# Query projection in halves of the array's rows, and sums in the output banks, in an attention kernel with two MLPs

## The chip, the cores and the metric

The kernel runs on one core of a Trainium2 chip. TensorE (PE) does the matmuls and writes to PSUM, which has eight banks of 512 float32 columns on 128 partitions; VectorE (DVE), ScalarE (ACT) and GpSimd (POOL) do the rest, and DMA queues, most of them issued by SyncE (SP), move data. Each engine works through its own list of instructions in order, and semaphores tell one of the others' progress. The metric is the device time of one execution in microseconds (us), lower is better.

## The reference

```python
def phi(x):                                   # q, k, v: (4, 8, 576, 64), w_phi: (64, 128)
    proj = np.einsum('bhsd,df->bhsf', x, w_phi)
    proj = proj - np.max(np.abs(proj), axis=-1, keepdims=True)
    return np.concatenate([np.exp(proj), np.exp(-proj)], axis=-1)
q_p, k_p = phi(q), phi(k)
kv = np.einsum('bhsf,bhsd->bhfd', k_p, v)
z = np.sum(k_p, axis=2)
num = np.einsum('bhsf,bhfd->bhsd', q_p, kv)
den = np.einsum('bhsf,bhf->bhs', q_p, z)[..., None] + 1e-06
attn_out = num / den                          # then (2304, 512): heads side by side
h = x @ w_in                                  # first MLP, 512 -> 2048 -> 512
x = np.maximum(0.01 * h, h) @ w_out
h = x @ w_in                                  # second MLP, with mish instead
x = (h * np.tanh(log1p(exp(h)))) @ w_out
```

The weights of the MLPs arrive as float64 and are turned into float32 on the chip, by integer operations on VectorE.

## The kernel before, in words

**Attention.** The 32 (batch, head) pairs are worked through two heads at a time, 16 units with index i. Of the 576 rows of a head 512 are the main part and 64 the left rest; the rests of several heads are put together. A head pair takes these steps, each with its own function: `transposes` brings queries and keys with the head dimension to the partitions (four 128x128 transposes each, even and odd rows on either half of the partitions; for an even i two more for the rests of two pairs); `split` makes of each a rounded high part (ScalarE, `hi`) and the remainder (VectorE, `lo`), so that `three` can multiply in three passes (lines 84 to 86). `q_proj` and `k_proj` project; the weight `wbd` has zeros on one half of its rows, so that a whole-array matmul picks the even or the odd rows. The queries come out with the features on the partitions: ScalarE copies them to `qd` (L403), GpSimd takes the maximum over the partitions (L408), `q_guard` subtracts it (L412). `k_guard` does it for the keys on VectorE (L365, L366). ScalarE makes the exponentials `kp`, `lp` (rests) and `qp`, each with either sign (L388). `kv` multiplies keys and values (L425, L428), with the column of ones that gives the sum; each matmul uses half of the array's columns, two are queued next to each other. `kv_copy` (L434) takes the sums out of the bank `kvp`. `nd` (L448, L453) makes numerators and denominators in the two banks `outs`; `normalise` (L461 to L464) divides on VectorE into `xn`, and `x_left` (L474) the left rows on ScalarE into `xleft`. `x_t` transposes `xn` into the bank `xt` (L482) and the left rows, by a matmul with two identities added, into a part of the next `kvp` (L484); ScalarE copies both to `X` (L485, L490).

**Order.** It is written out by hand: each engine works in the order in which the code issues. `attention(n)`, called turn n here, n = 0 to 16, works on five pairs at once: it normalises and transposes the outputs of pair x = n - 2, makes the outputs of o = n - 1, the exponentials and the sums of w = n, the projections of p = n + 1 and the input transposes of t = n + 2. In turn 15 the steps `moe(0)` and `moe(1)` of the first MLP are put in, in turn 16 and after it the third, and after that the MLPs run alone.

**PSUM.** Four banks are a ring, `bank("a")`, from which the projections and the input transposes take a bank in turn; `outs` has two banks, `kvp` one and `xt` one. For the MLPs the last four become the second ring.

**Conversion.** `Conv` turns one unit of weights (128x512) at a time. In turn n, `begin` clamps and shifts (L134, L136), `scale` multiplies on ScalarE (L150), `join` puts the bits together (L159, L162), and for the first ten units `split` in the next turn makes the two parts that stay in SBUF (L215, L216). Of the other 22 units of the first MLP five are converted in the turns and stored to HBM for later (`kept`, "store"), and fetched again in the first MLP block; the other 17 are converted there, by `step`, twice for each of the block's 14 items from item 2 on (L196, L198, L199, L205, L177, L215, L216).

**MLP.** For an item (128 hidden columns by 512 tokens) `emit_h` issues twelve matmuls, `leaky` makes the activation and its split (L663 to L670, `g`, `gh`, `gl`), and `emit_o`, two items later, twelve more.

Of the kernel before, what the change touches and what calls it, by code (L numbers as in the profile page):

```python
# [23 lines left out]
def attention_two_mlps_kernel(  # L24
# [12 lines left out]
    nc = tc.nc  # L37
# [18 lines left out]


    Q_COL = ((HM, 0, HM + P, P), (HM + LEFT, LEFT, HM + LEFT + P, LEFT + P))
# [160 lines left out]
    kept = rest[:17:4]  # L219
# [31 lines left out]
    with tc.manual_schedule():  # L251
# [3 lines left out]
        xleft = [ap.tile([P, 2, D], F32, name=f"xleft{i}", bufs=1) for i in range(2)]  # L255
        nc.vector.memset(xleft[0], 0.0)
# [8 lines left out]
        vleft = [ap.tile([P, 2, D + 1], F32, name=f"vleft{i}", bufs=1) for i in range(NV)]  # L265
        for i in range(NV):
            nc.vector.memset(vmain[i][:, :, :, D:D + 1], 1.0)
            nc.vector.memset(vleft[i], 0.0)
            for r in range(2):
                nc.vector.memset(vleft[i][r * LEFT:(r + 1) * LEFT, r, D:D + 1], 1.0)  # L270
        nc.vector.memset(xleft[1], 0.0)

        fold = ap.tile([P, LEFT], F32, name="fold", bufs=1)
        nc.vector.tensor_tensor(out=fold, in0=ident[:, 0:LEFT], in1=ident[:, LEFT:2 * LEFT], op=ALU.add)
# [3 lines left out]
        nc.vector.memset(outs[:, 0, 4 * (D + 1):5 * (D + 1)], 1.0)  # L278
# [30 lines left out]
        def values(i):  # L309
            b, p = divmod(i, NP)  # L310
            h0 = 2 * p
            vm = st[i]["vm"] = vmain[i % NV]
            for h in range(2):
                nc.sync.dma_start(out=vm[:, h, :, 0:D], in_=v[b, h0 + h, 0:MAIN, :].rearrange("(p t) d -> p t d", t=NM))
            vl = st[i]["vl"] = vleft[i % NV]
            for r in range(2):
                nc.sync.dma_start(out=vl[r * LEFT:(r + 1) * LEFT, r, 0:D], in_=v[b, h0 + r, MAIN:S, :])
# [5 lines left out]
        zeros = xleft[0].rearrange("p h d -> p (h d)")  # L323
# [6 lines left out]
        def transposes(i, *parts):  # L330

            s = st[i]
            l = lf[i // 2]
            for nm in parts or "qlk":
                if nm != "l":
                    t = bank("a")
                    for j in range(NM):  # L340
                        nc.tensor.transpose(
                            out=t[:, j * P:(j + 1) * P],
                            in_=s[nm + "n"].rearrange("p h t d -> p (h t d)")[:, j * P:(j + 1) * P], identity=ident)
                    n = HM if nm == "k" else HM + LEFT
                    hi, lo = (ap.tile([P, 2, n], F32R, tag=f"{nm}t{x}", name=f"{nm}t{x}", bufs=1) for x in "hl")
                    s[nm + "h"], s[nm + "l"] = (x.rearrange("p h n -> p (h n)") for x in (hi, lo))
                    split(hi[:, :, 0:HM], lo[:, :, 0:HM], t.rearrange("p (h n) -> p h n", h=2))
                elif i % 2 == 0:
                    t = bank("a")
# [5 lines left out]
                    split(l["h"], l["l"], t[:, 0:2 * P])  # L355

        def q_left(i):
            s, l = st[i], lf[i // 2]
            c = P + (i % 2) * LEFT
            for x in "hl":  # L360
                nc.vector.tensor_copy(out=s["q" + x][:, HM:HM + LEFT], in_=l[x][:, c:c + LEFT].bitcast(F32))
# [7 lines left out]
        def k_proj(i, c):  # L369
            s = st[i]  # L370
            if c == 0:
                s["kd"] = ap.tile([P, 2, NM, F], F32, tag="kd", name="kd")
            t = bank("a")
            for j in range(2):
                u = slice((2 * c + j) * P, (2 * c + j + 1) * P)
                three(t[:, j * 2 * F:(j + 1) * 2 * F], s["kh"][:, u], s["kl"][:, u], wbh, wbl)
            k_guard(t.rearrange("p (n f) -> p n f", f=F), NM, s["kd"][:, c])

        def k_proj_left(i):
            l = lf[i // 2]  # L380
            l["kd"] = ap.tile([P, 2, F], F32, tag="kdl", name="kdl", bufs=1)
            t = bank("a")
            three(t[:, 0:2 * F], l["h"][:, 0:P], l["l"][:, 0:P], wbh, wbl)
            k_guard(t[:, 0:2 * F].rearrange("p (n f) -> p n f", f=F), 2, l["kd"])
# [6 lines left out]
        def q_proj(i, c):  # L391
            s = st[i]
            h, o = divmod(c, 2)
# [3 lines left out]
            t = bank("a")  # L397
            n = HM + (h == o) * LEFT
            c0 = h * (HM + (1 - o) * LEFT)
            d0 = (1 - o) * (HM + h * LEFT)  # L400
            f = slice(o * F, (o + 1) * F)
            three(t[:, 0:n], wbh[:, f], wbl[:, f], s["qh"][:, c0:c0 + n], s["ql"][:, c0:c0 + n])
            nc.scalar.activation(out=s["qd"][:, h, d0:d0 + n], in_=t[:, 0:n], func=AF.Copy)  # L403
            half = s.setdefault("half", set())
            half.add(c)
            if {2 * h, 2 * h + 1} <= half:
                qd, qm = s["qd"][:, h, :], s["qm"][:, h, :]
                nc.gpsimd.partition_all_reduce(qm, qd, P, bass_isa.ReduceOp.absmax)  # L408
# [5 lines left out]
        def kv(i, a):  # L414

            s, l = st[i], lf[i // 2]
            if a == 0:
                s["kvp"] = pa.tile([P, 512], F32, tag="kvp", name="kvp")
            both = s["kvp"][:, 0:4 * (D + 1)].rearrange("p (h a n) -> p h a n", h=2, a=2)


            for h in range(2):
                for t in range(NM):
                    for r in HALVES:
                        nc.tensor.matmul(out=both[r, h, a, :], lhsT=s["kp"][a][:, h, t, r], rhs=s["vm"][:, h, t, :],  # L425
                                         start=(a == 0 and h == 0 and t == 0), stop=False, skip_group_check=True)
            for r in HALVES:
                nc.tensor.matmul(out=both[r, :, a, :], lhsT=l["lp"][a][:, i % 2, r], rhs=s["vl"],  # L428
                                 start=False, stop=(a == 1), skip_group_check=True)

        def kv_copy(i):
            s = st[i]
            s["kv"] = ap.tile([P, 4, D + 1], F32, tag="kv", name="kv", bufs=1)
            nc.scalar.activation(out=s["kv"], in_=s["kvp"][:, 0:4 * (D + 1)].rearrange("p (c n) -> p c n", n=D + 1), func=AF.Copy)  # L434

        def nd(i):

            s = st[i]
            N = D + 1
            t = s["nd"] = outs  # L440
            g = t[:, :, 0:4 * N].rearrange("p c (u h n) -> p c u h n", u=2, h=2)

            for u in range(NM):
                for h in range(2):
                    q0 = Q_COL[h][u]
# [5 lines left out]
            for a in range(2):  # L451
                for h, r in enumerate(HALVES):
                    nc.tensor.matmul(out=t[r, 1, 4 * N:5 * N], lhsT=s["qp"][a].rearrange("p h n -> p (h n)")[:, MAIN + r.start:MAIN + r.stop],  # L453
                                     rhs=s["kv"][:, 2 * h + a], start=(a == 0), stop=(a == 1))

        def normalise(i):
            s = st[i]
            N = D + 1
            t = s["nd"]
            den = s["den"] = ap.tile([P, 2, 5], F32, tag="den", name="den")  # L460
            nc.vector.tensor_scalar(out=den, in0=t[:, :, D:5 * N:N], scalar1=1e-6, scalar2=None, op0=ALU.add)  # L461
            nc.vector.reciprocal(out=den, in_=den)
            s["xn"] = ap.tile([P, NM, 2, D], F32, tag="xn", name="xn")
            nc.vector.tensor_tensor(  # L464
                out=s["xn"].rearrange("p (c u) h d -> p c (u h) d", c=2),
                in0=t[:, :, 0:4 * N].rearrange("p c (m n) -> p c m n", n=N)[:, :, :, 0:D],
                in1=den[:, :, 0:4].unsqueeze(3).to_broadcast([P, 2, 4, D]), op=ALU.mult)
            s["xl"] = xleft[i % 2]

        def x_left(i):  # L470

            s = st[i]
            for h, r in enumerate(HALVES):
                nc.scalar.activation(out=s["xl"][r, h], in_=s["nd"][r, 1, 4 * (D + 1):4 * (D + 1) + D], func=AF.Copy,  # L474
                                     scale=s["den"][r, 1, 4:5])

        def x_t(i):
            s = st[i]
            b, p = divmod(i, NP)
            t = pa.tile([P, 512], F32, tag="xt", name="xt")  # L480
            for j in range(NM):
                nc.tensor.transpose(out=t[:, j * P:(j + 1) * P], in_=s["xn"][:, j].rearrange("p h d -> p (h d)"), identity=ident)  # L482
            o = st[min(i + 1, PAIRS - 1)]["kvp"][:, MAIN - LEFT:MAIN]
            nc.tensor.matmul(out=o, lhsT=s["xl"].rearrange("p h d -> p (h d)"), rhs=fold, start=True, stop=True)  # L484
# [13 lines left out]
        def start():  # L498
# [6 lines left out]
            q_left(0)  # L505
            q_proj(0, 1)
            q_proj(0, 2)
            k_proj(0, 1)
            q_proj(0, 0)
            q_proj(0, 3)  # L510
# [8 lines left out]
        def attention(n):  # L519
# [23 lines left out]
            if w is not None:  # L543
                k_exp(w, 0)
# [24 lines left out]
            if p is None:  # L569
                normalise(o)  # L570
                x_left(o)
# [266 lines left out]
```

## Time and profile before

| | us |
|---|---|
| median of 3 runs | 969.28 (967.63 to 969.98) |
| the profiled execution | 967.76 |
| its span | 965.9 |
| TensorE busy | 950.6 (98%) |
| VectorE busy | 711.6 (74%) |
| ScalarE busy | 505.2 (52%) |
| GpSimd busy | 68.5 (7%) |

The span goes from the first to the last instruction that was profiled. Busy time is the union of an engine's instructions; matmuls overlap one another in the pipeline, so one lasts longer than the distance to the next, and it is the distances of starts that add up. Attention takes the first 182 us, the two MLPs the rest.

### The profile page before, as it was taken

The numbers are of one execution on the slowest core, as the hardware profiler recorded it, in microseconds if no ns is written. First come the engines' busy times: TensorE is split into PE (matmuls) and PEld (weight loads), VectorE is DVE, ScalarE is ACT, GpSimd is POOL, SyncE is SP. The second block draws the span as 40 slices with busy tenths as digits, with TensorE's granted clock in tenths as the row PEclk, the third lists the DMA queues.
The fourth block names the chain that finished last, engine by engine and source line by source line (L and its number), as shares of the span: only waits on it lengthen the run. The fifth ranks groups of instructions, "written<-read, shape, count | busy, mean of one in ns | idle before, by whom it ended". The sixth has DMA issues, their size and how long they took to land.

```text
span 965.9 us, 16740 instructions
## 1 busy us (share of the span) xinstructions
PE 950.6 (98%) x6704; PEld 813.9 (84%) x6704; DVE 711.6 (74%) x1271; ACT 505.2 (52%) x882; POOL 68.5 (7%) x36
## 2 busy tenths in 40 slices
PE   8999999999999999999999999999999999999998
PEld 7888999888888899888888888888888988888886
DVE  7999997599656575765344569778878689778875
ACT  6889998555433333432334456455445455445443
POOL 4433533000000000000000000000000000000000
PEclk9999999999999999999999999999999999999999
DMA  7444543255224444443012210001000100001001
GB/s 207 130 123 132 163 130 92 88 158 168 67 87 142 148 136 140 137 150 131 0 44 88 88 65 1 0 1 44 1 1 1 44 1 23 1 0 44 1 1 44
DMA packets 68206, 72.97 MB, mean 76 GB/s; under 512 B 27169, under 2 KB 52641, under 8 KB 68129
## 3 DMA queue, kind: packets, MB, share of 16 engines
q1 hardware_dynamic: 67392, 71.52, 23.8%
q8 instruction: 52, 0.85, 0.4%
q10 hardware_dynamic: 736, 0.39, 0.1%
q14 instruction: 26, 0.20, 0.1%
HBM read 57.48 MB, written 14.42 MB: 74 GB/s over the span
## 4 chain that ended last, share of the span: by engine, by line
PE 85%; DVE 9%; ACT 5%; POOL 1%; issue 1%; DMA 0%; POOLq 0%; ACTq 0%; DVEq 0%
PE a L84 14%; PE a L85 14%; PE a L86 14%; PE b L84 14%; PE b L86 14%; PE b L85 14%; DVE qd L412 1%; DVE mx L365 1%; ACT kp L388 1%; DVE kd L366 1%; DVE xn L464 1%; POOL qm L408 1%; ACT qp L388 1%; DVE wl L216 1%; PE outs L448 1%; PE kvp L425 1%
## 5 line engine op out<-in xcount | busy, mean ns | idle before, releaser
L84 PE MATMUL a<-wh,wh 128*128 128x512 f32 (+1 forms) x640 | 235.7, 368 | 0.0
L86 PE MATMUL a<-wh,wl 128*128 128x512 f32 (+1 forms) x640 | 235.4, 368 | 0.0
L85 PE MATMUL a<-wl,wh 128*128 128x512 f32 (+1 forms) x640 | 235.4, 368 | 0.0
L84 PEld LDWEIGHTS a<-wh,wh 128*128 128x128 f32 x640 | 120.6, 188 | 20.7 <-issue 0.3
L85 PEld LDWEIGHTS a<-wl,wh 128*128 128x128 f32 x640 | 120.7, 189 | 20.2
L86 PEld LDWEIGHTS a<-wh,wl 128*128 128x128 f32 x640 | 120.6, 188 | 20.0
L670 DVE TENSOR_TENSOR gl<-g,gh 128x512 fp32r<-128x512 f32 x72 | 49.9, 693 | 110.3 <-ACT gh L667 110.3
L84 PE MATMUL b<-gh,wh 128*128 128x512 f32 (+1 forms) x320 | 117.8, 368 | 0.8 <-ACT X L490 0.8
L85 PE MATMUL b<-gl,wh 128*128 128x512 f32 (+1 forms) x320 | 117.7, 368 | 0.0
L86 PE MATMUL b<-gh,wl 128*128 128x512 f32 (+1 forms) x320 | 117.7, 368 | 0.0
L84 PE MATMUL b<-wh,gh 128*128 128x512 f32 x288 | 112.2, 389 | 0.0
L85 PE MATMUL b<-wl,gh 128*128 128x512 f32 x288 | 112.2, 389 | 0.0
L86 PE MATMUL b<-wh,gl 128*128 128x512 f32 x288 | 112.1, 389 | 0.0
L667 ACT ACTIVATE gh<-g 128x512 fp32r<-128x512 f32 x72 | 45.5, 632 | 116.1 <-PE b L86 110.9
L692 ACT ACTIVATE gh<-u 128x512 fp32r<-128x512 f32 x72 | 45.5, 632 | 70.4 <-PE b L85 63.7
L666 DVE TENSOR_TENSOR g<-g,a 128x512 f32<-128x512 f32 x72 | 49.4, 687 | 42.8 <-ACT g L663 40.0
L408 POOL PARTITION_ALL_REDUCE qm<-qd x32 | 68.3, 2184 | 91.3 <-ACT qd L403 77.7
L719 ACT ACTIVATE r<-e,two 128x512 f32<-128x512 f32 x72 | 51.7, 718 | 36.3 <-DVE e L704 36.3
L84 PEld LDWEIGHTS b<-gh,wh 128*128 128x128 f32 x320 | 60.4, 189 | 10.9 <-ACT X L490 0.9
L86 PEld LDWEIGHTS b<-gh,wl 128*128 128x128 f32 x320 | 60.4, 189 | 10.0
L85 PEld LDWEIGHTS b<-gl,wh 128*128 128x128 f32 x320 | 60.3, 189 | 9.9
L688 ACT ACTIVATE e<-a 128x512 f32<-128x512 f32 x72 | 43.0, 597 | 47.9 <-PE a L86 26.6
(118 smaller groups left out, 1621.1 us busy)
## 6 DMA issues: line engine op xcount, KB each, us to landing
stage<-in_moe_w_in_dram SPq DMA_DIRECT2D x32, 512.0 KB, 3.8
stage<-in_moe_w_out_dram SPq DMA_DIRECT2D x32, 512.0 KB, 3.6
scr<-c SPq DMA_DIRECT2D x37, 256.0 KB, 2.0
wstage<-scr SPq DMA_DIRECT2D x32, 256.0 KB, 3.4
qn<-in_q_dram SPq DMA_DIRECT2D x16, 256.0 KB, 4.6
vmain<-in_v_dram SPq DMA_DIRECT2D x32, 128.0 KB, 3.5
kn<-in_k_dram SPq DMA_DIRECT2D x15, 256.0 KB, 4.3
out_dram<-X SPq DMA_DIRECT2D x15, 256.0 KB, 2.1
```

What stands on the lines that cost most here:

```text
L84: nc.tensor.matmul(out=o, lhsT=wh_, rhs=xh, start=start, stop=False)
L85: nc.tensor.matmul(out=o, lhsT=wh_, rhs=xl, start=False, stop=False)
L86: nc.tensor.matmul(out=o, lhsT=wl_, rhs=xh, start=False, stop=stop)
L216: return lambda: nc.vector.tensor_tensor(out=lo, in0=src, in1=hi.bitcast(F32), op=ALU.subtract)
L388: nc.scalar.activation(out=e, in_=src, func=AF.Exp, scale=float(sg))
L408: nc.gpsimd.partition_all_reduce(qm, qd, P, bass_isa.ReduceOp.absmax)
L666: nc.vector.tensor_tensor(out=g, in0=g, in1=h, op=ALU.max)
L667: nc.scalar.activation(out=hi, in_=g, func=AF.Copy)
L670: nc.vector.tensor_tensor(out=lo, in0=g, in1=hi.bitcast(F32), op=ALU.subtract)
L688: nc.scalar.activation(out=e0, in_=h0, func=AF.Exp)
L692: nc.scalar.activation(out=hi2, in_=u2, func=AF.Copy)
L719: nc.scalar.activation(out=r0, in_=e0, func=AF.Ln, bias=two)
```

## The change

- `q_proj` works on a whole head (both the even and the odd rows) in one call: six matmuls, of 64 rows of the array each, alternating between the upper half with one bank and the lower half with the other. One copy of 576 columns takes both out.
- A tile of two banks (`pair_of_banks`, one buffer) holds these projections, and also the transposes of queries and keys, which are split together, 1024 columns at once, into one tile `qk` for each part. In a turn three steps use it one after the other.
- `kv` writes its sums behind the outputs in the two `outs` banks instead of `kvp`, and the left rows' products use 64 rows by 64 columns of the array each, without zeros in `vleft`.
- `normalise` takes the left rows along (640 columns); `x_left` and its tiles are gone. `x_t` transposes the left rows by two matmuls of 64 rows by 64 columns into `outs`, and the rest into a bank of the ring; the bank `xt` is gone.
- In a turn the order is now first query head, `normalise`, keys, first exponential of the keys, second query head, left keys.
- Three units are stored for later instead of five; the two others are converted in the first MLP block.

```diff
@@ -54,8 +54,10 @@
-    Q_COL = ((HM, 0, HM + P, P), (HM + LEFT, LEFT, HM + LEFT + P, LEFT + P))
+    Q_COL = (0, HM + LEFT, P, HM + LEFT + P)
+    N = D + 1
+    KV0 = 5 * N
...
-    kept = rest[:17:4]
+    kept = rest[2:15:6]
...
+        def pair_of_banks():
+            return pa.tile([P, 2, 512], F32, tag="two", name="two").rearrange("p b n -> p (b n)")
+        qk = {x: ap.tile([P, 4, HM + LEFT], F32R, name=f"qk{x}", bufs=1) for x in "hl"}
...
+            both = None if parts else pair_of_banks()
             for nm in parts or "qlk":
+                g = "qk".find(nm)
                 if nm != "l":
-                    t = bank("a")
+                    t = bank("a") if parts else both[:, g * 2 * HM:(g + 1) * 2 * HM]
...
+            if not parts:
+                split(*(qk[x][:, :, 0:HM] for x in "hl"), both.rearrange("p (g n) -> p g n", n=HM))
...
-        def q_proj(i, c):
+        def q_proj(i, h):
...
+            at = []
+            t = pair_of_banks()
+            q0 = 512 - (HM + (1 - h) * LEFT)
+            for o in range(2):
+                n = HM + (h == o) * LEFT
+                c0 = h * (HM + (1 - o) * LEFT)
+                d0 = q0 + o * (HM + (1 - h) * LEFT)
+                at.append((t[:, d0:d0 + n], HALVES[o], slice(o * F, (o + 1) * F), slice(c0, c0 + n)))
+            for j, (w, x) in enumerate(((wbh, s["qh"]), (wbh, s["ql"]), (wbl, s["qh"]))):
+                for to, r, f, c in at:
+                    nc.tensor.matmul(out=to, lhsT=w[r, f], rhs=x[r, c], start=(j == 0), stop=(j == 2))
+            qd, qm = s["qd"][:, h, :], s["qm"][:, h, :]
+            nc.scalar.activation(out=qd, in_=t[:, q0:q0 + S], func=AF.Copy)
+            nc.gpsimd.partition_all_reduce(qm, qd, P, bass_isa.ReduceOp.absmax)
...
-            if a == 0:
-                s["kvp"] = pa.tile([P, 512], F32, tag="kvp", name="kvp")
-            both = s["kvp"][:, 0:4 * (D + 1)].rearrange("p (h a n) -> p h a n", h=2, a=2)
+            both = outs[:, :, KV0:KV0 + 2 * N].rearrange("p h (a n) -> p h a n", a=2)
...
             for r in HALVES:
-                nc.tensor.matmul(out=both[r, :, a, :], lhsT=l["lp"][a][:, i % 2, r], rhs=s["vl"],
-                                 start=False, stop=(a == 1), skip_group_check=True)
+                for h in range(2):
+                    nc.tensor.matmul(out=both[r, h, a, :], lhsT=l["lp"][a][HALVES[h], i % 2, r], rhs=s["vl"][HALVES[h]],
+                                     start=False, stop=(a == 1), skip_group_check=True)
...
-            s["xn"] = ap.tile([P, NM, 2, D], F32, tag="xn", name="xn")
+            s["xn"] = ap.tile([P, 2, 5, D], F32, tag="xn", name="xn")
...
-        def x_left(i):
-            s = st[i]
-            for h, r in enumerate(HALVES):
-                nc.scalar.activation(out=s["xl"][r, h], in_=s["nd"][r, 1, 4 * (D + 1):4 * (D + 1) + D], func=AF.Copy,
-                                     scale=s["den"][r, 1, 4:5])
...
-            t = pa.tile([P, 512], F32, tag="xt", name="xt")
+            t = bank("a")
...
-            o = st[min(i + 1, PAIRS - 1)]["kvp"][:, MAIN - LEFT:MAIN]
-            nc.tensor.matmul(out=o, lhsT=s["xl"].rearrange("p h d -> p (h d)"), rhs=fold, start=True, stop=True)
+            o = outs[:, 0, 4 * N:4 * N + LEFT]
+            for r in HALVES:
+                nc.tensor.matmul(out=o[r], lhsT=s["xn"][r, 1, 4], rhs=ident[r, r], start=True, stop=True)
...
             if p is not None:
-                for c in range(4):
-                    q_proj(p, c)
+                q_proj(p, 0)
             if x is not None and n < PAIRS:
                 normalise(x)
-                x_left(x)
             if p is not None:
                 for c in range(2):
                     k_proj(p, c)
+            if w is not None:
+                k_exp(w, 0)
+            if p is not None:
+                q_proj(p, 1)
                 if p % 2 == 0:
                     k_proj_left(p)
```

In the start the four query steps become `q_proj(0, 0)`, `k_proj(0, 1)`, `q_proj(0, 1)`, in this order, after `q_left(0)`.

## Rows read from the trace of the kernel before

**Rows 1.** Busy time of each engine in two stretches (start:end, length, busy us, clock, DMA).

```profile
95.70:116.10 20.40, 19.89 (x371) 18.46 (x369) 18.92 (x38) 18.83 (x38) 8.53 (x4) 1.00 0.50 141
182.50:255.00 72.50, 72.50 (x321) 60.02 (x320) 66.17 (x120) 39.95 (x70) 0.00 (x0) 1.00 0.45 138
```

**Rows 2.** VectorE in order of time, two turns: start, us, line, out<-in, idle before.

```profile
96.69 0.69 DVE L464 TENSOR_TENSOR xn<-outs,den 128x512 f32<-128x512 f32 x1
...
100.21 0.69 DVE L81 TENSOR_TENSOR qtl<-a,qth 128x512 fp32r<-128x512 f32 x1 [0.18 <-ACT qth L80]
...
106.12 0.69 DVE L216 TENSOR_TENSOR wl<-c,wh 128x512 fp32r<-128x512 f32 x1 [0.75 <-ACT wh L215]
...
117.13 0.69 DVE L464 TENSOR_TENSOR xn<-outs,den 128x512 f32<-128x512 f32 x1
```

**Rows 3.** ScalarE in order of time, the same two turns.

```profile
100.80 0.44 ACT L388 ACTIVATE lp<-kdl 128x256 f32<-128x256 f32 x1
...
107.91 0.63 ACT L474 ACTIVATE xleft<-outs,den 64x64 f32<-64x64 f32 x2 [0.61 <-DVE xn L464]
```

**Rows 4.** TensorE in order of time, turns 11 and 12 (xN merges N instructions).

```profile
129.42 0.61 PE L341 MATMUL a<-ident,qn 128*128 128x128 f32 x4
129.87 0.60 PE L341 MATMUL a<-ident,kn 128*128 128x128 f32 x4
130.40 2.09 PE L448 MATMUL outs<-kv,qp 128*64 128x65 f32 x64
...
134.64 0.39 PE L428 MATMUL kvp<-vleft,lp 128*64 128x130 f32 x4
134.96 0.41 PE L84 MATMUL a<-qth,wbh 128*128 128x320 f32 x1
135.21 0.30 PE L85 MATMUL a<-qtl,wbh 128*128 128x320 f32 x1
...
136.66 0.28 PE L84 MATMUL a<-wbh,kth 128*128 128x256 f32 x1
...
144.47 0.41 PE L84 MATMUL a<-qth,wbh 128*128 128x320 f32 x1
```

**Rows 5.** TensorE in order of time, turns 15 and 16.

```profile
165.42 0.60 PE L482 MATMUL xt<-ident,xn 128*128 128x128 f32 x4
...
166.12 2.09 PE L448 MATMUL outs<-kv,qp 128*64 128x65 f32 x64
...
169.46 1.15 PE L425 MATMUL kvp<-vmain,kp 128*64 128x65 f32 x32 [1.02 <-ACT X L485]
...
174.80 0.60 PE L482 MATMUL xt<-ident,xn 128*128 128x128 f32 x4
...
175.49 2.09 PE L448 MATMUL outs<-kv,qp 128*64 128x65 f32 x64
...
182.19 0.50 PE L84 MATMUL b<-gh,wh 128*128 128x512 f32 x1 [0.80 <-ACT X L490]
```

**Rows 6.** ScalarE in order of time, turn 16.

```profile
174.99 0.60 ACT L663 ACTIVATE g<-a 128x512 f32<-128x512 f32 x1 [1.69 <-PE a L86]
...
176.88 0.20 ACT L485 ACTIVATE X<-kvp 128x64 f32<-128x64 f32 x1
```

**Rows 7.** VectorE in order of time, first MLP block.

```profile
185.90 0.69 DVE L670 TENSOR_TENSOR gl<-g,gh 128x512 fp32r<-128x512 f32 x1 [2.56 <-ACT gh L667]
...
204.99 0.42 DVE L196 TENSOR_SCALAR c<-stage 128x512 f32<-128x512 f32 x1
...
207.79 0.68 DVE L666 TENSOR_TENSOR g<-g,a 128x512 f32<-128x512 f32 x1
...
250.12 0.69 DVE L670 TENSOR_TENSOR gl<-g,gh 128x512 fp32r<-128x512 f32 x1
```

**Rows 8.** TensorE in order of time, first MLP block.

```profile
253.04 0.39 PE L84 MATMUL b<-gh,wh 128*128 128x512 f32 x1
```

**Rows 9.** GpSimd in order of time, start of the kernel.

```profile
10.66 4.26 POOL L408 PARTITION_ALL_REDUCE qm<-qd  x2 [10.24 <-ACT qd L403]
```

More of the change, by code (lines that the diff above doesn't have):

```diff
@@ L254, in attention_two_mlps_kernel @@
         ident = ap.tile([P, P], F32, name="ident", bufs=1)
-        xleft = [ap.tile([P, 2, D], F32, name=f"xleft{i}", bufs=1) for i in range(2)]
-        nc.vector.memset(xleft[0], 0.0)
+        zeros = ap.tile([P, P], F32, name="zeros", bufs=1)
+        nc.vector.memset(zeros, 0.0)
         for r in range(2):
@@ L263, in attention_two_mlps_kernel @@
         vmain = [ap.tile([P, 2, NM, D + 1], F32, name=f"vmain{i}", bufs=1) for i in range(NV)]
-        vleft = [ap.tile([P, 2, D + 1], F32, name=f"vleft{i}", bufs=1) for i in range(NV)]
+        vleft = [ap.tile([P, D + 1], F32, name=f"vleft{i}", bufs=1) for i in range(NV)]
         for i in range(NV):
             nc.vector.memset(vmain[i][:, :, :, D:D + 1], 1.0)
[L268 to L274, printed above, removed]
+            nc.vector.memset(vleft[i][:, D:D + 1], 1.0)
         outs = pa.tile([P, 2, 512], F32, name="outs")
-        nc.vector.memset(outs[:, 0, 4 * (D + 1):5 * (D + 1)], 1.0)
+        nc.vector.memset(outs[:, 0, 4 * N:5 * N], 1.0)
+        def pair_of_banks():
+            return pa.tile([P, 2, 512], F32, tag="two", name="two").rearrange("p b n -> p (b n)")
+        qk = {x: ap.tile([P, 4, HM + LEFT], F32R, name=f"qk{x}", bufs=1) for x in "hl"}
         st = [dict() for _ in range(PAIRS)]
@@ L316, in values @@
             for r in range(2):
-                nc.sync.dma_start(out=vl[r * LEFT:(r + 1) * LEFT, r, 0:D], in_=v[b, h0 + r, MAIN:S, :])
+                nc.sync.dma_start(out=vl[r * LEFT:(r + 1) * LEFT, 0:D], in_=v[b, h0 + r, MAIN:S, :])
         for i in range(2):
@@ L336, in transposes @@
             l = lf[i // 2]
+            if not s.get("qh"):
+                s["qh"], s["ql"] = (qk[x].rearrange("p g n -> p (g n)") for x in "hl")
+                s["kh"], s["kl"] = (qk[x][:, 2:4] for x in "hl")
+            both = None if parts else pair_of_banks()
             for nm in parts or "qlk":
+                g = "qk".find(nm)
                 if nm != "l":
-                    t = bank("a")
+                    t = bank("a") if parts else both[:, g * 2 * HM:(g + 1) * 2 * HM]
                     for j in range(NM):
@@ L343, in transposes @@
                             in_=s[nm + "n"].rearrange("p h t d -> p (h t d)")[:, j * P:(j + 1) * P], identity=ident)
[L344 to L347, printed above, removed]
+                    if parts:
+                        split(*(qk[x][:, 2 * g:2 * g + 2, 0:HM] for x in "hl"), t.rearrange("p (h n) -> p h n", h=2))
                 elif i % 2 == 0:
-                    t = bank("a")
+                    t = bank("a")[:, 0:2 * P]
                     for j, x in enumerate(("kl", "ql")):
@@ L360, in q_left @@
             for x in "hl":
[L361 removed]
+                nc.vector.tensor_copy(out=qk[x][:, 0, HM:HM + LEFT], in_=l[x][:, c:c + LEFT].bitcast(F32))
         def k_guard(src, n, kd):
@@ L381, in k_proj_left @@
             l["kd"] = ap.tile([P, 2, F], F32, tag="kdl", name="kdl", bufs=1)
-            t = bank("a")
-            three(t[:, 0:2 * F], l["h"][:, 0:P], l["l"][:, 0:P], wbh, wbl)
-            k_guard(t[:, 0:2 * F].rearrange("p (n f) -> p n f", f=F), 2, l["kd"])
+            t = bank("a")[:, 0:2 * F]
+            three(t, l["h"][:, 0:P], l["l"][:, 0:P], wbh, wbl)
+            k_guard(t.rearrange("p (n f) -> p n f", f=F), 2, l["kd"])
         def exp(src, tag, sg):
@@ L396, in q_proj @@
                 s["qm"] = ap.tile([P, 2, S], F32, tag="qm", name="qm", bufs=1)
[L397 to L408, printed above, removed]
+            at = []
[12 more added lines that the diff above has]
+            nc.gpsimd.partition_all_reduce(qm, qd, P, bass_isa.ReduceOp.absmax)
         def q_guard(i):
@@ L452, in nd @@
                 for h, r in enumerate(HALVES):
-                    nc.tensor.matmul(out=t[r, 1, 4 * N:5 * N], lhsT=s["qp"][a].rearrange("p h n -> p (h n)")[:, MAIN + r.start:MAIN + r.stop],
+                    nc.tensor.matmul(out=outs[r, 1, 4 * N:5 * N], lhsT=s["qp"][a][:, h, HM:HM + LEFT],
                                      rhs=s["kv"][:, 2 * h + a], start=(a == 0), stop=(a == 1))
@@ L457, in normalise @@
             s = st[i]
[L458 to L461, printed above, removed]
+            den = ap.tile([P, 2, 5], F32, tag="den", name="den")
+            nc.vector.tensor_scalar(out=den, in0=outs[:, :, D:5 * N:N], scalar1=1e-6, scalar2=None, op0=ALU.add)
             nc.vector.reciprocal(out=den, in_=den)
-            s["xn"] = ap.tile([P, NM, 2, D], F32, tag="xn", name="xn")
+            s["xn"] = ap.tile([P, 2, 5, D], F32, tag="xn", name="xn")
             nc.vector.tensor_tensor(
[L465 to L468, printed above, removed]
-        def x_left(i):
-            s = st[i]
-            for h, r in enumerate(HALVES):
-                nc.scalar.activation(out=s["xl"][r, h], in_=s["nd"][r, 1, 4 * (D + 1):4 * (D + 1) + D], func=AF.Copy,
-                                     scale=s["den"][r, 1, 4:5])
+                out=s["xn"], in0=outs[:, :, 0:5 * N].rearrange("p c (m n) -> p c m n", n=N)[:, :, :, 0:D],
+                in1=den.unsqueeze(3).to_broadcast([P, 2, 5, D]), op=ALU.mult)
         def x_t(i):
```

32 lines of the change are left out of this document (12 added, 20 removed).

## The prediction

> **What bounds the kernel now.** I read the stretches first, then the waits of the attention turns, then the order of instructions on VectorE, ScalarE and TensorE, and last the hand-over to the MLPs. Two turns in mid-attention last 20.40 us, and in them TensorE is busy 19.89, VectorE 18.92 and ScalarE 18.83 [rows 1]: three engines are nearly full, so no single saving can shorten a turn by much. In the first block of the first MLP TensorE is busy for all 72.50 us and VectorE for 66.17 [rows 1]; there VectorE runs just behind TensorE. The granted clock is 1.00 in both.
>
> Which engine ends a turn is seen in VectorE's order. An even and an odd turn together take 20.44 us (one `xn` at 96.69, the next but one at 117.13), and VectorE idles only twice in them: 0.18 us for the query split's first half and 0.75 us for ScalarE's `wh` [rows 2]. The second comes at the end of an even turn because ScalarE is late: its queue reaches the work behind the key split only at 100.80 [rows 3]. From turn 12 on, when no converted weight is split any more, TensorE runs without a pause, 9.51 us from 134.96 to 144.47 [rows 4]. After 182.19 it hardly pauses again, so what attention gains or loses goes to the end unless the first MLP block changes it.
>
> **The change part by part.** The sum is made against the profiled execution's 967.76 us (span 965.9 and 1.9 around it), which lies 1.5 under the median 969.28. I add the sum to the median.
>
> *Query projection in halves of rows.* The twelve matmuls take 1.70 us (134.96 to 136.66) [rows 4]. They stay twelve, of the same columns, but each uses half the rows, and two neighbours use different halves and banks. No row shows row halves side by side. For column halves there is one: four transposes of 128 columns take 0.45 us (129.42 to 129.87), 0.88 ns a column, while 64 instructions of 65 columns on half the array's columns take 2.09, 0.50 ns a column [rows 4]. So halves can run two at a time. The bounds are 1.70 (one after the other) and 0.85; I take 0.85, the nearer case, a saving of 0.85 a turn.
>
> *More changes of the array's shape.* Going from whole-array matmuls to column halves, `outs` starts at 130.40, 0.08 us after four more transposes at 0.45 would be through; coming back, the first projection starts 0.09 late (four instructions of 0.057 after 134.64 would end at 134.87) and its successor comes 0.25 after it, where the twelve come 0.14 apart on average [rows 4]. Thus 0.27 us for a way in and out, 0.14 for each change. A turn has two such changes now and ten afterwards: into and out of the row halves twice, the left keys' quarter tiles within each half of `kv` and the quarter tiles of the left outputs. Eight more cost 1.1 us at 0.14; the bounds are 0.08 and 0.19 each, 0.6 to 1.5. The quarter tiles save about 0.1 (0.23 at 0.057 for four instructions of 130 columns now, eight of 65 after). TensorE's turn so becomes 9.51 - 0.85 - 0.10 + 1.12, or 9.7 us: nothing won there.
>
> The Trainium skill's page "TensorEngine Tiling (Array Packing)", section "Tiling Modes", says that tiles work independently, but that changing the tiling mode drains TensorE. The row above shows such a gap for column halves alone, and no run here shows one for row halves. By its first half alone the projection would fall to 0.85 and the turn to 8.6; with the second half it is the sum above.
>
> *The outputs' two banks shared.* `kv` and the left outputs' transpose now land in the banks from which `normalise` reads. The trace shows how banks are guarded: ScalarE's `xleft` read needs `den` alone, other columns than `xn` reads, and yet it sits idle 0.61 us until `xn` ends [rows 3]. So each access of another engine to these banks waits for the one before, whatever the columns: `normalise`, the left transpose, ScalarE's copy of it (L485), `nd`, `kv`, `kv_copy`, and again `normalise`. In turns 2 to 13 this chain has room, since the transposes (0.9 us) lie between the left transpose and `nd`, and VectorE comes to `normalise` after ScalarE's `wh`, which is queued behind `kv_copy`, anyway. It bites at the end, below.
>
> *ScalarE and VectorE in turns 2 to 11.* ScalarE loses two `xleft` copies (0.63 us) with their idle 0.61 [rows 3], and four query copies become two. VectorE's `xn` grows by 128 columns, 0.13 to 0.17 by 0.69 for 512 [rows 2]; one subtraction of 1024 columns for two of 512 saves about as little as one start. Even turn: after `xn` ends (97.38) TensorE needs 0.45 for four transposes, 0.4 for the left ones and their two changes, 1.1 for ten more transposes, and 0.2 pass before ScalarE starts (it starts `g` 0.19 after the transposes behind its source have begun [rows 5, 6]): 99.5. Its copy of 1024 columns ends near 100.4, against 100.80 now, and the queue behind it to `wh` is the same. So 0.4 of the 0.75 us goes. Odd turn: VectorE has no idle time and no less work: nothing. Five pairs give -2.0 us. Bounds: all the idle time of rows 2, -0.93 a pair or -4.7; and 0 if TensorE, waiting for the double bank that three steps share, takes over. I take -2.0, what the queue above gives.
>
> *Turns 12 to 14.* TensorE +0.17 each, and in turn 14, where no transposes cover it, `nd` waits about 0.2 for L485: +0.7 (from -2.0 at no cost of a change to +3.4 if the pairs don't overlap). The two conversions that go leave turns 14 and 15, where TensorE has no room to give back: 0.
>
> *Turns 15 and 16.* Here an MLP step stands ahead of the left outputs. Before, `nd` started at 166.12 and `kv` waited 1.02 us for L485; now `nd` waits. In turn 16 ScalarE's `g` starts 0.19 after the transposes at 174.80 have begun, and L485 1.89 after `g` [rows 5, 6]. With no `xleft` ahead of its exponentials ScalarE can do as well in turn 15: the transposes begin at 165.42, L485 ends at 167.7, `nd` starts 1.6 late, and `kv` no longer waits 1.0: +0.6. In turn 16 it started at 175.49 with nothing to wait for; L485 starts at 176.88 and takes 0.2 [rows 5, 6]: +1.65. The first MLP output waited 0.80 for the copy out of `xt`; now for the left copy alone, some 0.35 less [rows 5]. Together +1.3. Behind `nd` on TensorE are `kv` and the next MLP step, which everything waits for. If banks were not guarded whole, both would vanish, and 1.0 more: -1.35 instead of +1.9.
>
> *Two units converted later.* A unit costs VectorE 2.80 us with its split (204.99 to 207.79), a fetched one only the split, 0.6 to 0.8 [rows 7]. Two more make +4.0. Of that 0.7 (the first unit's clamp and shift) fits in the 2.56 us idle before 185.90, and I allow 0.3 more, as that is the one place in the stretch where VectorE waits long. So the `gl` of item 13, now 250.12 to 250.81 [rows 7], comes 3.0 later, and TensorE, which wants it at 253.04 [rows 8], has 2.2 of slack: +0.8 (0 to +1.8). Nothing refills it later.
>
> *Start.* GpSimd's first reduction starts at 10.66 [rows 9] and its chain paces the first two turns. Its copy is now 576 columns instead of 320, behind six matmuls instead of three: +0.3 (0.1 to 0.7). Fewer memsets free nothing that is waited for.
>
> **Sum**: 0.3 - 2.0 + 0.7 + 0.6 + 1.3 + 0.8 = +1.7 us, so 969.4 profiled and 971.0 as a median.
>
> **Rivals.**
> *Faster: latency goes all over.* Changes of shape cost 0.05, TensorE's turn falls to 8.9, VectorE's idle time [rows 2] goes almost wholly (-4.0), turns 12 to 14 give -1.7, the end still costs +1.9, block 0 +0.4, start +0.1: -3.3, 966.0. For it: VectorE's idle time is all somebody else's lateness. Against: the cheapest change of shape in the trace costs 0.08 [rows 4].
>
> *Slower: TensorE becomes the bound through shape changes.* At 0.19 each the turn is 9.51 - 0.95 + 1.5 = 10.1 (even) and 10.2 (odd), as long as the pair now: -0.5 for turns 2 to 11, +1.9 for 12 to 14, with +3.0 for the rest: +4.4, 973.7. It decides from 0.16 a change. For it: the first matmul after each change is itself drawn out. Against: row halves may load weights while others run.
>
> *Slower: the halves don't overlap*, the change doesn't do what it says. TensorE's turn is 10.5, a pair 21.3 against 20.44: +4.5, turns 12 to 14 +3.2, the rest +3.0: +10.7, 980. Against: the column halves do overlap.
>
> *Banks guarded by columns*: 3.2 less than the sum, 967.8; against it stands the idle 0.61 on ScalarE.
>
> **How the numbers follow.** A measurement of this kernel tells 0.3%, 2.9 us, from no change: 966.4 to 972.2. Forecast 0.33, its own range 968 to 973; banks by columns 0.12; faster rival 0.26; shape changes 0.20; no overlap 0.09. The forecast's upper end spills over 972.2 with 0.03 and the column case falls below 966.4 with 0.03; so faster 0.29, same 0.39, slower 0.32. Range 964.5 to 976.5: it takes in both bounds of the turns and leaves out the overlap failing and the best of the faster rival.
>
> **What would show it.** The two `nd` of turns 15 and 16 start some 1.6 us after the left transposes, with ScalarE's left copy as releaser; TensorE waits for the `gl` of item 13 in block 0; even turns shorten by 0.4 and odd ones not; the twelve projections take 0.9 us plus gaps of 0.1 to 0.2 at each change of shape. Wrong would be: `nd` starting straight after the transposes, a projection of 1.7 us, pairs of turns under 19.6 or over 20.8, or no wait in block 0.

## The result, and the profile after

The changed kernel takes 974.77 us (median of 4 runs, 974.64 to 975.31), the kernel before 969.16 beside it (967.63 to 969.98): a ratio of 1.0061, 95% interval 1.0043 to 1.0078, or 5.6 us slower. I had forecast 971.0, no difference that can be measured. The time lies in the range and on the side to which I had given 0.32. The profiled execution took 975.31 (span 973.2) against 967.76, so the two traces differ by 7.5, more than the medians; part of that lies in the start, below.

Where the traces part company is read from VectorE's `xn`, one in each turn: it stands at 32.92 in turn 2 before and at 36.44 after (+3.5), at 127.63 and 130.73 in turn 11 (+3.1). The first MLP output on TensorE comes at 182.19 and 188.59 (+6.4), and TensorE's last wait for VectorE in the first MLP block (block 0) makes it +7.1. So the start and the end of attention lost, and the turns between them gave back 0.4. VectorE in turn 2, before and after:

```profile
32.92 0.69 DVE L464 TENSOR_TENSOR xn<-outs,den 128x512 f32<-128x512 f32 x1
```

```profile
36.44 0.82 DVE L470 TENSOR_TENSOR xn<-outs,den 128x640 f32<-128x640 f32 x1
```

**Start.** TensorE of the kernel before in order of time (start, us, line, out<-in, idle before), up to its second and third query step:

```profile
7.36 0.36 PE L84 MATMUL a<-qth,wbh 128*128 128x256 f32 x1
...
8.44 0.39 PE L84 MATMUL a<-wbh,kth 128*128 128x256 f32 x1
8.66 0.28 PE L85 MATMUL a<-wbl,kth 128*128 128x256 f32 x1
8.78 0.28 PE L86 MATMUL a<-wbh,ktl 128*128 128x256 f32 x1
...
9.42 0.38 PE L84 MATMUL a<-qth,wbh 128*128 128x320 f32 x1
```

The same stretch of the changed kernel, TensorE:

```profile
7.91 0.42 PE L356 MATMUL a<-ident,ql 128*128 128x128 f32 x1
9.94 0.60 PE L415 MATMUL two<-qkh,wbh 64*128 64x320 f32 x2 [1.61 <-DVE qkl L368]
...
11.00 0.58 PE L86 MATMUL a<-wbh,qkh 128*128 128x256 f32 x1
11.38 0.41 PE L87 MATMUL a<-wbl,qkh 128*128 128x256 f32 x1
11.60 0.41 PE L88 MATMUL a<-wbh,qkl 128*128 128x256 f32 x1
```

and its VectorE, then GpSimd:

```profile
9.72 0.20 DVE L368 CAST qkl<-ll 128x64 fp32r<-128x64 f32 x1
12.69 0.69 DVE L372 TENSOR_REDUCE mx<-a 128x4 f32<-128x512 f32 x1 [2.77 <-PE a L88]
```

```profile
11.86 2.14 POOL L418 PARTITION_ALL_REDUCE qm<-qd  x1 [11.44 <-ACT qd L417]
14.53 2.14 POOL L418 PARTITION_ALL_REDUCE qm<-qd  x1 [0.52 <-ACT qd L417]
19.27 4.26 POOL L418 PARTITION_ALL_REDUCE qm<-qd  x2 [2.60 <-DVE qd L422]
```

The old quarter at 7.36 has 256 columns: no left rows. The new step takes a whole head, 320 columns with the left rows in them, and these pass through TensorE's `L356`, ScalarE's `lh` and VectorE's casts before the first matmul may start: 2.0 us lie between 7.91 and 9.94. Queued behind it on TensorE are the second keys (11.00 instead of 8.44), so VectorE's `mx` comes late, and GpSimd's two reductions, which ran from 10.66 without a gap [rows 9], begin at 11.86 and stand 0.52 apart. The matmuls of 256 columns also come 0.21 apart up to 15.2, and 0.12 apart before from 6.75 on.

**Turns 2 to 11.** The two turns that answer to [rows 1], and block 0 (same columns):

```profile
100.02:120.39 20.37, 20.00 (x391) 17.42 (x391) 19.10 (x36) 17.48 (x28) 8.53 (x5) 1.00 0.51 140
188.50:262.00 73.50, 73.19 (x321) 60.10 (x322) 67.58 (x124) 39.72 (x71) 0.00 (x0) 1.00 0.47 147
```

ScalarE's busy time fell from 18.83 to 17.48, VectorE's rose from 18.92 to 19.10, and the pair shortened only from 20.44 to 20.37. VectorE shows why; against [rows 2] part of its idle time has moved, and its own work fills the rest:

```profile
100.02 0.82 DVE L470 TENSOR_TENSOR xn<-outs,den 128x640 f32<-128x640 f32 x1
...
104.16 1.23 DVE L83 TENSOR_TENSOR qkl<-two,qkh 128x1024 fp32r<-128x1024 f32 x1 [0.33 <-ACT qkh L82]
...
109.31 0.69 DVE L218 TENSOR_TENSOR wl<-c,wh 128x512 fp32r<-128x512 f32 x1 [0.39 <-ACT wh L217]
...
120.39 0.82 DVE L470 TENSOR_TENSOR xn<-outs,den 128x640 f32<-128x640 f32 x1
```

ScalarE in the even turn, first the kernel before (`xn` at 96.69), then the changed one (`xn` at 100.02):

```profile
105.43 0.66 ACT L215 ACTIVATE wh<-c 128x512 fp32r<-128x512 f32 x1
```

```profile
103.10 1.03 ACT L82 ACTIVATE qkh<-two 128x1024 fp32r<-128x1024 f32 x1
104.02 0.41 ACT L395 ACTIVATE lp<-kdl 128x256 f32<-128x256 f32 x1
...
108.65 0.64 ACT L217 ACTIVATE wh<-c 128x512 fp32r<-128x512 f32 x1
```

Counted from `xn`, ScalarE's `wh` starts at 8.74 before and 8.63 after, only 0.11 earlier. The even turn shortened by 0.14 (10.49 to 10.35), the odd one grew by 0.07 (9.95 to 10.02).

**Turns 12 to 16 and block 0.** TensorE, which answers to [rows 4, 5, 8]:

```profile
135.64 1.10 PE L433 MATMUL outs<-vmain,kp 128*64 128x65 f32 x32
136.67 0.34 PE L438 MATMUL outs<-vleft,lp 64*64 64x65 f32 x8
136.95 1.15 PE L433 MATMUL outs<-vmain,kp 128*64 128x65 f32 x32
...
138.31 0.41 PE L415 MATMUL two<-qkh,wbh 64*128 64x320 f32 x2
138.53 0.33 PE L415 MATMUL two<-qkl,wbh 64*128 64x256 f32 x2
138.65 0.36 PE L415 MATMUL two<-qkh,wbl 64*128 64x256 f32 x2
...
148.11 0.41 PE L415 MATMUL two<-qkh,wbh 64*128 64x320 f32 x2
...
162.24 2.08 PE L456 MATMUL outs<-kv,qp 128*64 128x65 f32 x64 [0.33 <-ACT X L484]
...
170.44 0.33 PE L483 MATMUL outs<-ident,xn 64*64 64x64 f32 x4
172.26 2.09 PE L456 MATMUL outs<-kv,qp 128*64 128x65 f32 x64 [1.49 <-ACT X L484]
...
182.28 2.09 PE L456 MATMUL outs<-kv,qp 128*64 128x65 f32 x64 [1.48 <-ACT X L484]
...
188.59 0.50 PE L86 MATMUL b<-gh,wh 128*128 128x512 f32 x1 [0.32 <-ACT X L484]
...
260.25 0.50 PE L87 MATMUL b<-gl,wh 128*128 128x512 f32 x1 [0.22 <-DVE gl L666]
```

Row halves do run side by side: a pair of 320 and 256 columns starts 0.12 after the one before it, which is the distance of single matmuls of 256. A turn without conversions still grew from 9.51 to 9.80 (138.31 to 148.11). In turns 15 and 16 `nd` waits for the left copy, as forecast, and so does the first MLP output; the four waits are 3.62 us together.

### The profile page after: what moved, and what is told of

Same layout as the page of the kernel before. It is cut to its first block, busy times and chain, and to the rows that moved or that the text cites. A ratio compares the mean times of both kernels' runs of the same rounds, so it can differ in the third digit from the quotient of the medians.

```text
span 973.2 us, 16949 instructions
## 1 busy us (share of the span) xinstructions
PE 956.8 (98%) x6864; PEld 808.1 (83%) x6864; DVE 711.3 (73%) x1249; ACT 493.0 (51%) x804; POOL 68.5 (7%) x36
## 4 chain that ended last, share of the span: by engine, by line
PE 83%; DVE 12%; ACT 3%; issue 1%; DMA 1%; ACTq 0%; DVEq 0%
PE a L86 13%; PE a L87 13%; PE a L88 13%; PE b L87 12%; PE b L88 12%; PE b L86 12%; DVE wl L218 2%; PE outs L456 2%; PE outs L433 2%; DVE c L179 1%; DVE e L207 1%; ACT wh L217 1%; PE two L348 1%; PE two L415 1%; DVE qd L422 1%
```

## The experiments

Each was timed in five rounds beside the kernel before; their ratios are to it, and a difference from the changed kernel is one of medians. The theory: the start lost by its order, the end by the shared banks, block 0 by the two units; the rival: TensorE lost by changes of shape in every turn. (A change of shape is a step of TensorE from one division of its array into tiles to another.)

**The start's old order in the changed kernel** (`q_part` is the old quarter step on all rows, writing into the new tiles):

```diff
-            q_proj(0, 0)
+            q_part(0, 1)
+            q_part(0, 2)
             k_proj(0, 1)
-            q_proj(0, 1)
+            q_part(0, 0)
+            q_part(0, 3)
```

> The changed kernel, with the first pair's queries projected as before: four whole-array steps, two of them ahead of the left rows. If the order of the start costs the 3.5 us by which the first normalisation came later (36.44 instead of 32.92), that normalisation returns to about 33 and the time falls by 3 to 3.5 us, to some 971.5. If the late start was chance of the one profiled execution, or came with the row halves anyway, nothing changes (within 0.7 us of 974.8).

972.99 us (971.42 to 976.7), ratio 1.0046 (1.0032 to 1.0060): -1.8, with the first `xn` at 34.66. It gains less than expected. In its profiled execution the matmuls come 0.21 apart until 12.3, so that trace still bears the slower spacing. And part of the gain went again in block 0, by waits for `gl`: from the first MLP output to the last instruction it takes 784.97 instead of 784.63.

**The new order in the kernel before:**

```diff
+            q_proj(0, 0)
             q_proj(0, 1)
-            q_proj(0, 2)
             k_proj(0, 1)
-            q_proj(0, 0)
+            q_proj(0, 2)
             q_proj(0, 3)
```

> The kernel before, with the first pair's query steps in the order of the changed kernel: none ahead of the left rows. If the order of the start is what costs (TensorE has nothing to do for 1.6 us, the first reduction starts later and matmuls come at the slower spacing), the first normalisation comes 1.5 to 3.5 us later than at 32.92 and the time rises as much, to 970.6 to 972.6. If it is the row halves and the double bank, the time stays at 969.1 within 0.7.

971.41 us (970.98 to 971.93) against 969.01, ratio 1.0025 (1.0015 to 1.0036): +2.4. Its TensorE makes the same wait with whole-array matmuls, one bank each:

```profile
7.95 0.42 PE L351 MATMUL a<-ident,ql 128*128 128x128 f32 x1
9.98 0.60 PE L84 MATMUL a<-qth,wbh 128*128 128x320 f32 x1 [1.61 <-DVE qtl L361]
```

and GpSimd starts at 12.27 and 15.04. So the order alone does it, not row halves or the double bank. In this profiled execution, its slowest (971.93), the first `xn` stands at 37.01, 4.1 later than before and more than expected.

**All left outputs into a bank of the ring:**

```diff
-            o = outs[:, 0, 4 * N:4 * N + LEFT]
+            o = bank("a")[:, 0:LEFT]
```

> The changed kernel, with the left outputs transposed into a bank of the ring instead of the outputs' bank. If nd waits because a bank is guarded whole, the waits of 0.33, 1.49 and 1.48 us ahead of nd in turns 14, 15 and 16 go, and the time falls by about 3.2 us, to 971.6. If the MLP step's activation ahead of it is what holds nd, the waits stay and so does the time (974.8).

974.81 us (974.43 to 978.13), ratio 1.0070 (1.0056 to 1.0084): no gain. The waits of `nd` are gone, but the ring has four banks and five users in a turn now, and the left transpose waits for the second keys' subtraction:

```profile
113.16 0.66 PE L480 MATMUL a<-ident,xn 128*128 128x128 f32 x4
114.58 0.33 PE L483 MATMUL a<-ident,xn 64*64 64x64 f32 x4 [0.76 <-DVE kd L373]
```

Its pairs take 21.02 (101.92 to 122.94), 0.65 more. From the first `xn` to the first projection of turn 12 that adds up to 3.5 (36.35 to 141.69, instead of 36.44 to 138.31), as much as the next run gains at the end.

**The same for the last four pairs only** (`if i < 12` keeps the old place), where the ring is less used:

> The changed kernel, with the left outputs of the last four pairs transposed into a bank of the ring, those of the others into the outputs' bank as in the changed kernel. If whole-bank guarding costs the waits of 0.33, 1.49 and 1.48 us and only the fifth use of the ring in every turn ate up the gain when all left outputs went there, the time falls by 3.0 to 3.3 us, to 971.6. If the ring is short of banks here too, or something else holds turns 15 and 16, it falls by under 1 us.

971.27 us (970.96 to 973.02), ratio 1.0029 (1.0018 to 1.0041): -3.5, about the sum of the four waits (3.62). TensorE goes straight on:

```profile
170.03 0.33 PE L483 MATMUL a<-ident,xn 64*64 64x64 f32 x4
170.29 2.09 PE L456 MATMUL outs<-kv,qp 128*64 128x65 f32 x64
```

**Five units stored for later, not three** (`kept = rest[:17:4]`):

> The changed kernel, with five units converted in the turns and stored, as before. If block 0 lost 0.75 us to the two further conversions and turns 14 and 15 have room for them, the time falls by 0.7 us, to 974.1, and TensorE no longer waits for gl in block 0. Rival: the two conversions lengthen turns 14 and 15 by up to 2 us each and the time rises, to 976 or more.

973.79 us (973.65 to 974.39), ratio 1.0050 (1.0038 to 1.0062): -1.0, and no wait for `gl` in block 0. From the first MLP output to the last instruction its trace takes 783.70, the kernel before 783.68; the traces with three units take 784.60 to 785.44, which is open. Turn 14 keeps its length (8.96), so the rival is out.

**The query projection on all rows** (`lhsT=w[:, f], rhs=x[:, c]`), order and banks as changed:

> The changed kernel, with the query projection on all rows of the array (the weights have zeros in the other half), same banks and same copies. By the sum of gaps: the twelve take 1.70 us again instead of 1.27, and four changes of shape a turn go, about 0.33: turns 12 to 14 (TensorE without a pause, 9.80 and 9.99 from one first projection to the next) change by 0.1 each, the total by 0 to +1 us. If the row halves are a clear gain that the changes of shape don't eat up, turns 12 to 14 grow by 0.4 to 0.85 each and pairs of turns may follow, +1.5 to +8 us.

976.53 us (976.2 to 976.77), ratio 1.0077 (1.0065 to 1.0089): +1.8. That is more than the sum of gaps allowed and in the range of the other theory. Its pairs of turns still take 20.37, with TensorE busy for 20.34 of it, so in turns 2 to 11 row halves are worth nothing, if barely. Elsewhere they gain: the first `xn` comes at 37.07 instead of 36.44, turn 12 takes 10.11 (139.06 to 149.17) instead of 9.80, and from there to the first MLP output it takes 0.66 more (139.06 to 190.00, instead of 138.31 to 188.59).

**The left keys' products over all rows** (zeros in `vleft` again). It takes three changes of shape out of a turn: into and out of the quarter tiles in the first half of `kv`, and into them in the second; one change to the row halves stays behind it. (The expectation counted two.)

```diff
-   ...lhsT=l["lp"][a][HALVES[h], i % 2, r], rhs=s["vl"][HALVES[h]],
+   ...lhsT=l["lp"][a][:, i % 2, r], rhs=s["vl"][:, h],
```

> The changed kernel with the products of the left keys taken over all 128 rows (the rows past the left ones filled with zeros) instead of over a part of them, so that two changes of shape a turn fall away on TensorE. Theory (the matmuls' change of shape costs about 0.1 us each where TensorE is the bound): only turns 12 to 16 gain, some 0.3 to 0.8 us in all, 973.9 to 974.5. Rival (changes of shape cost nothing that the end sees): 974.4 to 975.2, even with the changed kernel.

974.38 us (973.86 to 976.04), ratio 1.0057 (1.0043 to 1.0071), which doesn't tell the two theories apart. The trace does: from the first projection of turn 12 to the first MLP output TensorE takes 49.66 (137.39 to 187.05) instead of 50.28 (138.31 to 188.59), 0.62 less, as the theory had it. The median hides it, since block 0 took it back: TensorE waited there for `gl` twice (before 253.28 and 259.52), and from the first MLP output to the last instruction it took 785.44 instead of 784.63. Why it waited more there stays open.

**Four more matmuls of zeros ahead of the first query step**, to fill TensorE's idle 1.61:

> The changed kernel, with four matmuls of zeros more, ahead of the first pair's queries, where TensorE has nothing to do for 1.6 us. If it is TensorE's slower spacing in the start (256 columns in 0.21 us up to 16 us) that costs, and the idle time brings it, the spacing is 0.12 from about 10 us on, and the time falls by 1 to 1.5 us, to 973.5. If the order alone costs, nothing changes (974.8 within 0.5) or it rises by the time of the added matmuls, up to 0.7.

976.78 us (975.49 to 977.53), ratio 1.0082 (1.0070 to 1.0094): +2.0, a miss. The spacing was 0.12 from 6.67 on, but after an idle 1.46 at 14.42 it fell to 0.21 further on. In the busy times by stretch the granted clock is the third figure from the end:

```profile
14.50:15.00 0.50, 0.30 (x2) 0.10 (x2) 0.50 (x2) 0.00 (x0) 0.50 (x1) 1.00 0.25 56
15.00:15.50 0.50, 0.33 (x2) 0.33 (x4) 0.44 (x3) 0.00 (x0) 0.07 (x1) 0.72 0.48 85
15.50:18.00 2.50, 2.50 (x13) 2.18 (x12) 2.30 (x4) 1.90 (x3) 0.36 (x1) 0.50 0.98 335
```

Its profiled execution was its fastest and lasts as long as that of the changed kernel: the first `xn` comes 0.5 earlier (35.95), and block 0 takes that back with a second wait for `gl` (before 254.10; 785.24 from the first MLP output to the last instruction).

Its other four runs, 1.3 to 2.0 us slower, had a mean granted clock of 0.996 to 0.997 instead of 0.998, so they spent longer at the low level; where isn't seen, and the rest stays open.

**Old start, left outputs of the last four pairs in the ring, five units kept:**

> Three edits to the changed kernel together: the old start, the last left outputs in the ring, five units stored. If their gains add (1.8, 3.2 and 1.0 us, from 974.8), it comes to 968.8, even with the kernel before within 0.7 us. If the conversions left in turns 14 and 15 collide with the shorter turns, or TensorE's gain there is taken back in block 0, it stays over 970.5.

967.77 us (966.65 to 972.02), ratio 0.9992 (0.9983 to 1.0002): 7.0 below the changed kernel, where the three alone gave 1.8 + 3.5 + 1.0 = 6.3. That it is more fits block 0: with five units it takes nothing back (783.69 from the first MLP output to the last instruction).

**The same with the left keys' products over all rows:**

> The old order of the first pair's steps, the last four pairs' left outputs in the ring, five stored units kept, and the left keys' products over all rows. Theory (changes of shape cost where TensorE is the bound): 967.0 to 967.5, below the kernel with the first three alone (967.8). Rival (they cost nothing that the end sees): 967.6 to 968.2, even with it.

966.84 us (965.63 to 968.32), ratio 0.9976 (0.9967 to 0.9985), below the kernel before by 2.3 us: its interval excludes no change, though the gain is within the 0.3% that I had called no difference. From the run above its median differs by 0.9. From the first projection of turn 12 to the first MLP output the traces differ by 0.63 (45.76 and 46.39), which is the edit; the first `xn` (32.76 and 33.86) differs by the pace of the two starts, which the edit doesn't touch. Its turn 12 lasts 9.64 instead of 9.80, and `kv` in it:

```profile
141.56 1.10 PE L454 MATMUL outs<-vmain,kp 128*64 128x65 f32 x32
142.49 0.45 PE L459 MATMUL outs<-vleft,lp 128*64 128x65 f32 x8
142.72 1.15 PE L454 MATMUL outs<-vmain,kp 128*64 128x65 f32 x32
143.66 0.45 PE L459 MATMUL outs<-vleft,lp 128*64 128x65 f32 x8
144.04 0.41 PE L417 MATMUL two<-qkh,wbh 64*128 64x320 f32 x2
```

That is 2.48 from the first to the projection, 2.67 in the changed kernel (135.64 to 138.31): three changes fewer save 0.19. But the 0.19 is what is left of more: the left products give up running side by side. The eight take 0.23 here (142.49 to 142.72); in the changed kernel four start within 0.02 of one another, so the eight would take about half, 0.11 to 0.12. With some 0.12 given up in each half of `kv`, a change costs (0.19 + 0.24) / 3 = 0.14 us, an estimate. Two middle turns keep their length:

```profile
96.30:116.67 20.37, 19.75 (x394) 17.50 (x391) 19.09 (x36) 17.38 (x28) 8.54 (x5) 1.00 0.49 139
```

TensorE is busy 0.25 less than in the changed kernel, and the pair lasts exactly as long; TensorE's one wait of a pair, for `xn`, grew instead (0.53 before 97.18, and 0.37 before 100.91 in the changed kernel). With the run on all rows, where TensorE was busy 0.34 more, that settles the rival: TensorE doesn't bound turns 2 to 11. That VectorE's order with its waits for ScalarE does is read from the rows; no run made either lighter.

## Why the prediction was right, and where not

That the time lies in the range is owed to the range's width of 12 us: the sum gave +1.7 and the result is +5.6.

*The start is the term that was mis-sized*: +0.3, where the traces differ by 3.5 and the medians by 1.8 (undone in the changed kernel) to 2.4 (done in the one before). I priced the step by its own length, a longer copy and three more matmuls ahead of it, and took its place in the queue as unchanged. I did not ask which of its inputs comes last. The left rows were a rest that only two of four old steps needed; the whole-head step needs them at once, and the keys stand behind it.

*Turns 2 to 11*: -2.0 forecast, -0.4 measured. The even turn's wait for `wh` did fall from 0.75 to 0.39, by the 0.4 forecast, but for another reason. I had ScalarE's copy end 0.4 earlier and its whole queue with it. The rows show the work behind the copy reached at 4.00 after `xn` instead of 4.11, and `wh` 0.11 earlier. The rest of the fall is VectorE's own lateness: its `xn` grew by 0.13, which I had counted and not charged, and it waits 0.15 longer at the split (0.18 to 0.33), since ScalarE's single copy of 1024 columns must end before VectorE may begin, where it used to begin after the first 512. In the odd turn, where no wait for `wh` was left to fall, that added work lengthened the turn.

*Turns 12 to 14*: +0.7 forecast, +1.1 measured, as the steps from 134.96 to 162.57 before became 138.31 to 167.06. The overlap is real: the twelve projections take 0.63 and 0.64 up to the next step's first matmul (138.31 to 138.94, 140.56 to 141.20), 1.27 instead of 1.70, not counting the changes into them. A change of shape cost what I had put, 0.14, or a little more; each of these is an estimate from the traces. By `kv` it is the 0.14 above. By the whole turn it is 0.155: with free changes my terms leave 9.51 - 0.85 - 0.10 = 8.56, it takes 9.80, and there are eight more. By the run on all rows it is 0.18: there three changes go and the 0.85 of overlap with them, and turn 12 takes 0.31 more. So turns 12 and 13 grew by 0.29 and 0.30 instead of 0.17; in turn 14 the wait of `nd` was 0.33 instead of 0.2, and it grew by 0.55. The Trainium skill, page "TensorEngine Tiling (Array Packing)", section "Tiling Modes", says that a change of mode drains TensorE; the trace agrees: behind a change to row halves the next pair starts 0.22 later (138.31 to 138.53), the one after it 0.12.

*Turns 15 and 16*: +0.6 and +1.3 forecast. From one turn to the next TensorE took 0.67 and 1.24 more, with the releaser that I had named. The 0.32 at the MLP hand-over was forecast too. Undoing it, together with the 0.33 of turn 14, gave 3.5, more than 1.9, since the waits of before ([rows 5]: 1.02 and 0.80) went with it.

*Block 0*: +0.8 forecast, 0.95 in the trace (784.63 instead of 783.68 from the first MLP output to the last instruction), -1.0 when undone. The `gl` of item 13 came 2.98 later, counted from the first MLP output, where I had 3.0.

So the sum came out 3.9 us low in medians: some 1.5 to 2.1 by the start, 1.6 by the middle turns, 0.4 by turns 12 to 14. The rival of the shape changes named nearly the time (973.7), and its price for a change (from 0.16) is near the estimates above; but TensorE's turns 12 and 13, without conversions, add up to 19.79, below the pair of 20.37, so it never became the bound. No overlap and banks by columns are refuted by the rows above, the faster rival by the 0.4 that turns 2 to 11 gave.

The traces differ by 7.5 and the medians by 5.6. The kernel before ran 967.6 to 970.4 in all its runs here, and the profiled one was among the fastest. Traces of other runs with the same start tell how much of the 3.5 is the order. Where matmuls come 0.12 apart from 6.7 us on, the first `xn` stands at 32.92 and 32.76 with the old order (the kernel before, the run with four edits) and at 35.87 and 35.74 with the new one (five units, left keys over all rows): 2.8 to 3.1 for the order. Where they come 0.21 apart from the beginning, it is 33.86 and 34.66 against 36.35 to 36.47: 1.7 to 2.6. So of the 3.5 some 0.6 is the slower start of the changed kernel's profiled execution, and the rest goes with the order.

## What to carry to other kernels

When small steps are merged, look for the input that comes last among all their inputs, and for what is queued behind the merged step: at a kernel's start the old order may have been what hid it. Price an engine's relief only where that engine's lateness ends a wait, and charge the other engine's added work against the same gap. The banks that several engines share cost nothing here while work lay between the accesses, so look at the last turns, where that work has run out.

## What had not been expected of the hardware

The start depends on the execution. Matmuls of 256 columns came 0.21 apart up to 15.2 us in the changed kernel, up to 12.3 and 10.2 in two experiments with the old order (its first experiment, and the one with three edits together), and 0.12 apart from 6.7 on in a third (the one with four edits). The granted clock reads 1.00 throughout in the first three; where a fall is recorded (0.50, the 1.2 GHz level, between 15.5 and 18 above) the distance is the same 0.21. So at the start the distance of matmuls told the clock better than its column. The Trainium skill, page "TensorE: Matmul & The Clock Gate", part "The HAM clock gate", says that the number of matmuls at the low clock at a kernel's start varies from run to run; these traces agree.

The wait that the new order opens brings the low level even where the start had the high one. In the run with the left keys over all rows TensorE's matmuls came 0.12 apart up to its last transposes; then it had nothing to do for 1.8 us, the granted clock fell to 0.50 in that time, and the distance was 0.21 up to 14.6:

```profile
7.26 0.27 PE L358 MATMUL a<-ident,ql 128*128 128x128 f32 x1
9.35 0.60 PE L417 MATMUL two<-qkh,wbh 64*128 64x320 f32 x2 [1.81 <-DVE qkl L370]
```

```profile
8.00:9.00 1.00, 0.00 (x0) 0.00 (x0) 0.97 (x3) 0.00 (x0) 0.00 (x0) 0.73 0.86 286
...
9.50:14.00 4.50, 4.50 (x23) 3.62 (x24) 1.38 (x2) 1.30 (x2) 2.21 (x2) 0.50 0.77 199
```

The run with five units shows the same. The old order, in the run with four edits, kept 0.12 throughout. Of two executions that differ by a microsecond or two, the start is the first place to compare.
